# Hash attention with a max-out feed-forward on one core: token order, load runs, and which queue carries which transfer when

## The chip, the cores and the metric

One core of a Trainium2 chip. The metric is the device time of the whole program in microseconds (us); every time below is such a time or a duration in the trace of one profiled execution. A ratio between two kernels is the mean time of one kernel's runs over the mean of the other's runs of the same rounds, so it is not quite the ratio of the medians quoted beside it. PE is the matmul engine, PEld its weight loads; DVE, ACT and Pool are the vector, scalar and general engines; SP only issues DMAs. The granted clock is the share of PE's full clock that it was given.

## The reference

Attention with a bucket mask, then a feed-forward network (FFN) with a maximum of three products. B = 4, H = 8, S = 768, D = 64; 3072 tokens of 512 values, inner width 768.

```python
q_bits = (np.einsum('bhsd,dk->bhsk', q, proj) > 0)      # 6 hash bits for each token and head
k_bits = (np.einsum('bhsd,dk->bhsk', k, proj) > 0)
mask = q_bucket[:, :, :, None] == k_bucket[:, :, None, :]    # bucket = the 6 bits as a number
scores = np.where(mask, scale * np.matmul(q, k.transpose(0, 1, 3, 2)), -1e9)
attn = softmax(scores)
x = (attn @ v) laid out as (B*S, H*D)
h = np.maximum(np.maximum(x @ w1, x @ w2), x @ w3)
out = h @ w_out
```

## The kernel before

The program has 16 phases, one for each batch and pair of heads, and each phase has 12 units. A unit is two matmuls of q and k (one for each head) and one exp on ACT. A unit also carries small jobs from a list `todo[u]`. In phase n these are: the denominators and the product with v of phase n-1, the hash of pair n+1, the transposes of pair n+2, and the loads of pair n+3. Pieces of the FFN come from a queue (`ffn`) as fast as a quota allows. They can exist only once a batch has all four pairs.

The mask costs no pass over the scores. Twelve extra rows in the bf16 operands of each head (`kop`, `qop`) hold the hash bits and their complements, so that the matmul itself adds a large negative number for each differing bit. These rows are made for the next pair by a matmul (L237), turned into bits by DVE (`bt`) and moved to their rows by eight small DMAs of 12 partitions. They are called **row DMAs** below. The next phase can't start before its rows have landed.

```python
def load(nm, b, j):                       # q or k of a pair, three phases ahead
    t = natp.tile([P, R * D], FP32, ...)  # R = 24
    if b == 0:                            # two heads interleaved by 64 columns: runs of 256 bytes
        for hd in (0, 1):
            nc.sync.dma_start(t[:, 0:S].rearrange("p (c x) -> p c x", c=NCH)[:, :, D*hd : D*hd + D],
                              src[b, 2*j + hd].rearrange("(p c) d -> p c d", p=P))
    else:                                 # other batches: another token order, runs of 6016 bytes
        ...  nc.sync.dma_start(t[32*g : 32*g + 32, 0 : R*D - 32], ...)     # four for each tensor

def pe_transpose(nm, b, j, half, evac):   # batch 0 only; later batches are transposed on DVE
    for c in range(NT3):
        nc.tensor.transpose(ps[:, c*P : c*P + P], nat[nm, b, j][:, o : o + P], iden[:])

def hash_pair(b, j):                      # the row DMAs, on the queue of SP
    ...
    nc.vector.tensor_scalar(out=bt[:, half_cols(half)], in0=ps[half][:, 0:HS], ...)   # the bits
    for hd in (0, 1):
        for z, nm in enumerate(("q", "k")):
            nc.sync.dma_start(oset(b, j)[nm, hd][12 hash rows, half_cols(half)], bt[12 rows, ...])

def den_rc(ph): ...                       # denominators; eight small copies on Pool
def load_weight(i, after):                # a whole weight (768 KB) on Pool, held until `after` is written
    nc.gpsimd.tensor_copy(gate[:], after)
    nc.gpsimd.dma_start(t[:], w_ap...)

# the places (ph = phase, u = unit; cut)
ul = 7 if ph == 0 else 0
add(ul, load, "k", nb, nj); add(ul, load, "q", nb, nj)        # pair ph + 3
if nb > 0: add(9, load_v, nb, nj)                             # four DMAs on Pool
if ph == 0: add(8, load_weight, 0, ...)
if ph == 1: add(4, load_weight, 1, ...); add(10, load_weight, 2, ...)
if ph == 2: add(8, load_weight, 3, ...)                       # w_out
add(1, hash_pair, *pairs[ph + 1])
...
# after all units of a phase: FFN of a batch is queued one phase after its last pair
if ph > 0 and pairs[ph - 1][1] == NPAIR - 1:
    for half in (0, 1): ffn.extend(ffn_atoms(pairs[ph - 1][0], half))
```

The softmax here doesn't subtract the row's maximum and nothing guards it: scores larger than these inputs give would overflow.

Of the kernel before, what the change touches and what calls it, by code (L numbers as in the profile page):

```python
# [9 lines left out]
FP32 = mybir.dt.float32  # L10
FP16 = mybir.dt.float16
# [6 lines left out]
def kernel(  # L18
# [29 lines left out]
    TINY = 1.1754943508222875e-38  # L48

    konst = ctx.enter_context(tc.tile_pool(name="konst", bufs=1))  # L50
    natp = ctx.enter_context(tc.tile_pool(name="natp", bufs=2))
    tfp = ctx.enter_context(tc.tile_pool(name="tfp", bufs=2))
    vp = ctx.enter_context(tc.tile_pool(name="vp", bufs=5))
# [21 lines left out]
    nat = {}  # L75
    HBM = {"k": k, "q": q}

    def load(nm, b, j):
        src = HBM[nm]
        t = natp.tile([P, R * D], FP32, tag=nm + "nat", name=nm + "nat")  # L80
        if b == 0:
            for hd in (0, 1):
                nc.sync.dma_start(t[:, 0 : S].rearrange("p (c x) -> p c x", c=NCH)[:, :, D * hd : D * hd + D],
                                  src[b, 2 * j + hd].rearrange("(p c) d -> p c d", p=P))
        else:
            for hd in (0, 1):
                s = src[b, 2 * j + hd].rearrange("(i r) d -> i (r d)", r=R)
                for blk in (0, 1):
                    g = 2 * hd + blk
                    nc.sync.dma_start(t[32 * g : 32 * g + 32, 0 : R * D - 32],  # L90
                                      s[:, 32 * blk : 32 * blk + R * D - 32])
        nat[nm, b, j] = t

    def load_first():
        for nm in ("k", "q"):
            nat[nm, 0, 0] = natp.tile([P, R * D], FP32, tag=nm + "nat", name=nm + "nat")
        for half in (0, 1):
            for nm, eng in (("k", nc.sync), ("q", nc.scalar)):
                t3 = nat[nm, 0, 0][:, 0:S].rearrange("p (c x) -> p c x", c=NCH)
                for hd in (0, 1):  # L100
                    eng.dma_start(t3[:, half * NT3 : half * NT3 + NT3, D * hd : D * hd + D],
                                  HBM[nm][0, hd].rearrange("(p c) d -> p c d", p=P)[:, half * NT3 : half * NT3 + NT3, :])

    vt = {}

    def load_v(b, j):
        t = vp.tile([P, 2, NCH, D], FP16, tag="v", name="v")
        tv = t[:].rearrange("p h c d -> p h (c d)")
        sv = v[b, 2 * j : 2 * j + 2]
        if b == 0:  # L110
            nc.gpsimd.dma_start(tv, sv.rearrange("h (p c) d -> p h (c d)", p=P))
        else:
            s4 = sv.rearrange("h (i jj c) d -> jj i h (c d)", jj=4, c=NCH)
            for jj in range(4):
                nc.gpsimd.dma_start(tv[32 * jj : 32 * jj + 32], s4[jj])  # L115
        vt[b, j] = t

    pr = konst.tile([P, NBITS], FP32, name="pr")
    nc.gpsimd.dma_start(pr[0:D], proj[:, :])
    nc.gpsimd.dma_start(pr[D : 2 * D], proj[:, :])  # L120
    load_first()


    iden = konst.tile([P, P], FP32, name="iden")
# [46 lines left out]

    at = [konst.tile([P, 2, HS + 1], FP16, name=f"at{i}") for i in range(4 * NCH)]
    gate = konst.tile([P, 1], FP32, name="gate")
    w_sb = []

    def load_weight(i, after):
        nc.gpsimd.tensor_copy(gate[:], after)
        w_ap = (moe_w1, moe_w2, moe_w3, moe_w_out)[i]
        t = konst.tile([P, w_ap.shape[0] // P, w_ap.shape[1]], FP16, name=f"w{i}_sb")
        nc.gpsimd.dma_start(t[:], w_ap.rearrange("(c p) f -> p c f", p=P))  # L180
        w_sb.append(t)


    def psum2(name):
# [9 lines left out]
    def pe_transpose(nm, b, j, half, evac):  # L194
        if (nm, b, j) not in tf:
            tf[nm, b, j] = tfp.tile([P, S], FP32, tag=nm + "tf", name=nm + "tf")
        ps = bank()
        for c in range(NT3):
            o = half * HS + c * P
            nc.tensor.transpose(ps[:, c * P : c * P + P], nat[nm, b, j][:, o : o + P], iden[:])  # L200
        evac(tf[nm, b, j][:, half_cols(half)], ps[:, 0:HS])  # L201

    def transpose(nm, b, j):
        tf[nm, b, j] = tfp.tile([P, S], FP32, tag=nm + "tf", name=nm + "tf")
        dst = tf[nm, b, j][:]
        src = nat[nm, b, j][:].rearrange("p (r x) -> p r x", x=D)[:, :, 0:32]
        if nm == "q":
            nc.vector.transpose(dst.rearrange("p (r i) -> p r i", i=32), src)  # L208
        else:
            nc.vector.transpose(dst.rearrange("p (c jj i) -> p c jj i", jj=4, i=32),  # L210
                                src.rearrange("p (jj c) x -> p c jj x", jj=4))

    def convert(nm, b, j, cs=slice(0, S), copy=nc.vector.tensor_copy):
        for hd in (0, 1):
# [35 lines left out]
    def atile(ph, half, c):  # L250
        return at[(ph % 2) * 2 * NCH + 2 * c + half]
# [9 lines left out]
        nc.scalar.activation(atile(ph, half, c)[:, :, 0:HS], sc[:, :, 0:HS], ActFn.Exp, scale=SCALE)  # L261

    rcb = {}
    E32 = HS // 32

    def den_mm(ph, c0, c1):
# [39 lines left out]
    def av(ph, b, j, half):  # L306
        ps = bank()
        vv = vt[b, j]
        for c in range(NCH):
            for hd in (0, 1):  # L310
                nc.tensor.matmul(ps[D * hd : D * hd + D, 0 : HS + 1], vv[:, hd, c, :],  # L311
                                 atile(ph, half, c)[:, hd, :], start=(c == 0), stop=(c == NCH - 1))
        sv = dp.tile([P, 1], FP32, tag="sv", name="sv")
        nc.vector.tensor_scalar(out=sv[:], in0=ps[:, HS : HS + 1], scalar1=EPS, scalar2=None, op0=AluOp.mult)  # L314
        if b not in xT:
            xT[b] = xp.tile([P, NJC, S], FP16, tag="xT", name="xT")
        nc.vector.scalar_tensor_tensor(
            out=xT[b][:, j, half * HS : half * HS + HS], in0=ps[:, 0:HS],
            scalar=sv[:, 0:1], in1=rcb.pop((ph, half))[:], op0=AluOp.add, op1=AluOp.mult)


    hts = {}

    def l1(b, half, fb, m):
        ps = bank()
        for jc in range(NJC):
            nc.tensor.matmul(ps[:, 0:HS], w_sb[m][:, jc, fb * P : fb * P + P],  # L327
                             xT[b][:, jc, half * HS : half * HS + HS],
                             start=(jc == 0), stop=(jc == NJC - 1))
        if m == 0:  # L330
# [9 lines left out]
    def l2(b, half, t):  # L340
        ps = bank()
        for fb in range(NFB):
            nc.tensor.matmul(ps[:, 0:DM], hts[b, half, fb][:, t * P : t * P + P], w_sb[3][:, fb, :],  # L343
                             start=(fb == 0), stop=(fb == NFB - 1))
        if t == 0:
            ot[b, half] = op.tile([P, NT3, DM], FP32, tag="o", name="o")
        o = ot[b, half]
        nc.scalar.copy(o[:, t, :], ps[:, 0:DM])  # L348
        ob = out[b * S : b * S + S]
        c0 = half * NT3  # L350
        last = b == B - 1 and half == 1
        if b == 0:
            if t == NT3 - 1:
                nc.gpsimd.dma_start(ob.rearrange("(p t) m -> p t m", t=NCH)[:, c0 : c0 + NT3, :], o[:])
        elif t == NT3 - 1 or last:
            ts = slice(t, t + 1) if last else slice(0, NT3)
            o4 = ob.rearrange("(i c jj) m -> jj i c m", c=NCH, jj=4)
            for jj in range(4):
                eng = (nc.sync if jj % 2 == 0 else nc.scalar) if last else nc.gpsimd
                eng.dma_start(o4[jj][:, c0 + ts.start : c0 + ts.stop, :], o[32 * jj : 32 * jj + 32, ts, :])  # L360

    def ffn_atoms(b, half):
        for fb in range(NFB):
# [5 lines left out]

    pairs = [(b, j) for b in range(B) for j in range(NPAIR)]  # L370
    NU = 2 * NCH
    ffn = deque()
    ffn_left = [2 * B * (3 * NFB * 0.65 + NT3 * 1.28)]
    TAILW = 40.0

# [9 lines left out]
    hash_first("q", 0)  # L385
    convert("q", 0, 0, h0, acopy)
    pe_transpose("k", 0, 0, 1, vcopy)
    for j in (1, 2):
        load("k", 0, j)
        load("q", 0, j)  # L390
    load_v(0, 0)
    for t in at:
        nc.gpsimd.memset(t[:, :, HS : HS + 1], 1.0)

    for ph, (b, j) in enumerate(pairs):
        todo = {u: [] for u in range(NU)}

        def add(u, f, *a):
            todo[u].append(lambda: f(*a))
# [12 lines left out]
        if ph > 0:  # L412
# [7 lines left out]
            add(5, den_rb, ph - 1, 1)  # L420
            add(6, av, ph - 1, pb, pj, 0)
            add(8 if sparse else 6, av, ph - 1, pb, pj, 1)
        if ph + 3 < len(pairs):
            nb, nj = pairs[ph + 3]
            ul = 7 if ph == 0 else 0
            add(ul, load, "k", nb, nj)
            add(ul, load, "q", nb, nj)
            if nb > 0:
                add(9, load_v, nb, nj)
        if ph == 0:  # L430
            add(8, load_v, 0, 1)
            add(8, load_weight, 0, nat["q", 0, 2][:, 0:1])
        if ph == 1:
            add(4, load_weight, 1, atile(ph, 0, 1)[:, 0, 0:1])
            add(8, load_v, 0, 2)
            add(10, load_weight, 2, atile(ph, 0, 4)[:, 0, 0:1])
        if ph == 2:
            add(4, load_v, 0, 3)
            add(8, load_weight, 3, atile(ph, 0, 3)[:, 0, 0:1])
        if ph == 0:  # L440
            pass
        elif ph + 1 < len(pairs):
            add(1, hash_pair, *pairs[ph + 1])
        if ph + 2 < len(pairs):
            prep(*pairs[ph + 2], 8)
# [14 lines left out]
        for c, half in order:  # L460
# [9 lines left out]
                spent += cost  # L470
            ffn_left[0] -= spent
            u += 1
        if ph > 0 and pairs[ph - 1][1] == NPAIR - 1:
            for half in (0, 1):
                ffn.extend(ffn_atoms(pairs[ph - 1][0], half))

    lph = len(pairs) - 1
    tailf = [lambda: den_mm(lph, 0, NCH), lambda: den_rc(lph), None, None, lambda: den_rb(lph, 0), lambda: den_rb(lph, 1),
# [5 lines left out]
            ffn.popleft()[1]()  # L484
    while ffn:
        ffn.popleft()[1]()
    for half in (0, 1):
        for _, f in ffn_atoms(B - 1, half):
            f()


# [28 lines left out]
```

## Time and profile before

| | before |
|---|---|
| median, range | 311.2 us, 309.87 to 311.26 (3 runs) |
| profiled execution: span, mean granted clock | 310.3 us, 0.964 |
| PE busy | 281.6 us, 91% of the span |
| packets under 512 bytes | 17088 of 29631 |

The first fence is part 2 of the page of the kernel before: the span in 40 slices of 7.76 us, each digit a busy share in tenths; PEclk is the granted clock of PE, DMA the share of the 16 DMA engines.

```profile
PE   6686848478899999999999999999999999999993
PEclk9996978879999999999999999999999999999998
DMA  8687999995873738482856476630400030030303
```

From slice 12 on PE is full. Whatever is to be won lies in the first 11 slices, which are phases 0 to 4: no FFN work exists yet to fill PE, and the clock sinks too. The second fence is the windows view, one row for each of phases 0 to 4 (from the phase's first exp to the next phase's). Its columns are window and length, busy time of PE, PEld, DVE, ACT and POOL with instruction counts, then granted clock, DMA share and GB/s. (It counts a packet's whole time where the packet starts, and packets can overlap, so the share can pass 1.)

```profile
10.60:26.80 16.20, 11.28 (x76) 5.80 (x77) 12.64 (x25) 9.37 (x13) 3.35 (x5) 0.95 0.65 111
26.80:44.00 17.20, 13.29 (x101) 5.41 (x100) 9.10 (x19) 9.54 (x13) 6.34 (x17) 0.80 1.06 209
44.00:58.20 14.20, 11.27 (x88) 3.95 (x89) 6.65 (x14) 9.39 (x14) 5.25 (x15) 0.82 1.02 197
58.20:75.60 17.40, 10.93 (x88) 3.97 (x88) 8.89 (x18) 9.32 (x14) 3.55 (x12) 0.80 0.77 153
75.60:87.10 11.50, 9.65 (x90) 4.05 (x90) 8.94 (x18) 9.30 (x15) 3.55 (x12) 1.00 0.77 159
```

Phase 4 takes 11.5 us. Phases 1 to 3 have about the same work on ACT (9.3 to 9.5 us) and take 48.8 us together. The chain of waits (the work that ended last, followed back from the end, each piece to what released it) of the kernel before says what fills the difference (start, length, what; times in us):

```profile
1.97 3.69 DMA pr<-in_proj_dram
...
20.35 5.28 DMA kop_1_159<-bt
...
28.45 1.46 PE wk L237 x16
...
39.80 5.44 DMA kop_2_165<-bt
45.25 9.58 DMA qnat<-in_q_dram
54.85 0.72 SPq L246
55.61 7.59 DMA qop_0_151<-bt
```

Four waits, three for row DMAs and one for a load of q, make up 27.9 us. Not all of this is lost: engines work meanwhile, and phases 1 to 3 are 14.3 us longer than three phases of 11.5 us. A row DMA holds only 9 KB, so it isn't its size that makes it slow. The SP timeline of the kernel before shows the first reason, what stands before the rows on SP's queue (start, length, SP's issues by line, what, how many):

```profile
25.80 1.30 SPq L83 DMA_DIRECT2D knat<-in_k_dram  x2
27.21 1.27 SPq L83 DMA_DIRECT2D qnat<-in_q_dram  x2
28.58 2.91 SPq L90 DMA_DIRECT2D knat<-in_k_dram  x4
31.60 3.33 SPq L90 DMA_DIRECT2D qnat<-in_q_dram  x4
35.61 0.80 SPq L246 DMA_DIRECT2D qop_2_166<-bt  x1
```

The bits of this pair were computed by DVE from 29.98 on, the first half of them by 30.66. The first row went out at 35.61, 5.0 us later, behind eight load issues that took SP 6.2 us. The q load in the chain holds a row back too: SP stood 0.43 us until it had landed, and then issued the row at 54.85.

The second reason is what the rows meet on the DMA engines. From each row DMA's issue to the end of its last packet (worked out from the packet records of the trace) it took 4.2 to 5.2 us in phase 1 and 2.6 to 6.3 us in phase 2, while the DMA share was above 1.

The DMA view of the kernel before for the window from 3 to 9 us, when batch 0 is being loaded:

```profile
DMA packets 5373, 1.33 MB, mean 222 GB/s; under 512 B 5356, under 2 KB 5373, under 8 KB 5373
```

The PE timeline, six transposes of 128x128 in the transpose mode of PE, which is one tensor of one pair:

```profile
20.32 0.82 PE L200 MATMUL wk<-iden,knat 128*128 128x128 f32 x6
```

### The profile page before, as it was taken

The numbers are of one execution on the slowest core, as the hardware profiler recorded it, in microseconds if no ns is written. First come the engines' busy times: TensorE is split into PE (matmuls) and PEld (weight loads), VectorE is DVE, ScalarE is ACT, GpSimd is POOL, SyncE is SP. The second block draws the span as 40 slices with busy tenths as digits, with TensorE's granted clock in tenths as the row PEclk, the third lists the DMA queues.
The fourth block names the chain that finished last, engine by engine and source line by source line (L and its number), as shares of the span: only waits on it lengthen the run. The fifth ranks groups of instructions, "written<-read, shape, count | busy, mean of one in ns | idle before, by whom it ended". The sixth has DMA issues, their size and how long they took to land.

```text
span 310.3 us, 6166 instructions
## 1 busy us (share of the span) xinstructions
PE 281.6 (91%) x2184; PEld 144.1 (46%) x2184; DVE 194.6 (63%) x409; ACT 191.4 (62%) x286; POOL 75.9 (24%) x250
## 2 busy tenths in 40 slices
PE   6686848478899999999999999999999999999993
PEld 2331412123345554555455545554555455555551
DVE  3884544628697884688478857876796253725250
ACT  3573745548776668666868596868676776141412
POOL 8230612303404040404040415040301040120200
PEclk9996978879999999999999999999999999999998
DMA  8687999995873738482856476630400030030303
GB/s 170 126 130 155 211 222 221 153 211 103 160 189 55 201 47 228 98 196 41 207 132 156 74 188 155 165 70 4 111 2 9 2 104 1 2 90 11 90 15 103
DMA packets 29631, 35.73 MB, mean 115 GB/s; under 512 B 17088, under 2 KB 24928, under 8 KB 29600
## 3 DMA queue, kind: packets, MB, share of 16 engines
q1 hardware_dynamic: 18784, 22.75, 31.3%
q0 software_dynamic: 8928, 11.80, 20.3%
q10 hardware_dynamic: 1888, 0.79, 1.2%
q8 instruction: 17, 0.28, 0.4%
q14 instruction: 14, 0.11, 0.1%
HBM read 34.21 MB, written 6.29 MB: 131 GB/s over the span
## 4 chain that ended last, share of the span: by engine, by line
PE 79%; DMA 10%; DVE 4%; ACT 3%; issue 2%; ACTq 1%; SPq 1%; POOL 0%; DVEq 0%; POOLq 0%
PE wk L327 31%; PE sc L259 18%; PE wk L311 10%; PE wk L343 9%; PE wk L274 6%; PE wk L237 4%; DMA qnat<-in_q_dram 3%; DMA qop_0_151<-bt 2%; DMA kop_2_165<-bt 2%; DMA kop_1_159<-bt 2%; DMA pr<-in_proj_dram 1%; PE wk L222 1%; DVE ktf L201 1%; ACT o L348 1%; ACTq L360 1%
## 5 line engine op out<-in xcount | busy, mean ns | idle before, releaser
L327 PE MATMUL wk<-xT,w_sb 128*128 128x384 f16 x576 | 110.8, 326 | 0.0
L327 PEld LDWEIGHTS <-w_sb 128*128 128x128 f16 x576 | 54.1, 97 | 45.1 <-issue 9.8
L240 DVE TENSOR_SCALAR bt<-wk,thrqk,fac 128x384 bf16<-128x384 f32 x30 | 18.9, 672 | 36.1 <-PE wk L237 32.1
L259 PE MATMUL sc<-qop_0_151,kop_0_149 128*128 128x384 bf16 x72 | 23.7, 329 | 4.9 <-DMA qop_0_151<-bt 4.6
L311 PEld LDWEIGHTS <-v 128*64 128x64 f16 x384 | 20.6, 110 | 13.7 <-issue 6.4
L259 PE MATMUL sc<-qop_0_154,kop_0_153 76*128 76x384 bf16 x72 | 23.6, 328 | 3.4 <-DVE qop_0_154 L226 1.0
L259 PE MATMUL sc<-qop_1_160,kop_1_159 76*128 76x384 bf16 x60 | 20.4, 339 | 5.6 <-DMA kop_1_159<-bt 2.9
L115 POOL DMA_DIRECT2D v<-in_v_dram x48 | 25.4, 540 | 0.0
L259 PE MATMUL sc<-qop_2_166,kop_2_165 76*128 76x384 bf16 x60 | 20.0, 334 | 3.8 <-DMA kop_2_165<-bt 2.1
L348 ACT COPY o<-wk 128x512 f32<-128x512 f32 x24 | 14.0, 585 | 14.5 <-PE wk L343 14.4
L360 POOL DMA_DIRECT2D out_dram<-o x20 | 10.8, 549 | 47.7 <-ACT o L348 47.7
L259 PE MATMUL sc<-qop_2_163,kop_2_161 128*128 128x384 bf16 x60 | 20.1, 335 | 2.2 <-DMA qop_2_163<-bt 1.1
L259 PE MATMUL sc<-qop_1_157,kop_1_155 128*128 128x384 bf16 x60 | 20.2, 337 | 0.1
L274 PEld LDWEIGHTS <-ones_143 128*32 128x32 f16 x384 | 8.9, 99 | 17.6 <-issue 14.8
L237 PE MATMUL wk<-qtf,pmq 64*32 64x384 f32 x120 | 15.8, 564 | 0.0
L285 DVE STREAM_TRANSPOSE dT<-ds 128x384 f32<-128x384 f32 x16 | 9.2, 572 | 9.6 <-ACT ds L280 9.6
L237 PE MATMUL wk<-ktf,pmk 64*32 64x384 f32 x120 | 14.7, 564 | 0.0
L261 ACT ACTIVATE at_174<-sc 128x768 f16<-128x768 f32 x8 | 6.5, 814 | 11.5 <-PE sc L259 11.5
L314 DVE TENSOR_SCALAR sv<-wk 128x1 f32<-128x1 f32 x32 | 4.9, 153 | 12.3 <-PE wk L311 12.3
L261 ACT ACTIVATE at_169<-sc 128x768 f16<-128x768 f32 x8 | 6.5, 814 | 9.5 <-PE sc L259 9.5
L261 ACT ACTIVATE at_181<-sc 128x768 f16<-128x768 f32 x8 | 6.5, 814 | 8.9 <-PE sc L259 8.9
L208 DVE STREAM_TRANSPOSE qtf<-qnat 128x768 f32<-128x768 f32 x12 | 11.7, 975 | 0.2
(469 smaller groups left out, 641.2 us busy)
## 6 DMA issues: line engine op xcount, KB each, us to landing
knat<-in_k_dram SPq DMA_DIRECT2D x48, 188.0 KB
qnat<-in_q_dram SPq DMA_DIRECT2D x48, 188.0 KB
out_dram<-o POOLq DMA_DIRECT2D x20, 192.0 KB, 3.6
w_sb<-in_moe_w_dram POOLq DMA_DIRECT2D x3, 768.0 KB, 8.9
v<-in_v_dram POOLq DMA_DIRECT2D x48, 48.0 KB, 2.8
out_dram<-o POOLq DMA_DIRECT2D x2, 768.0 KB, 6.2
knat<-in_k_dram SPq DMA_DIRECT2D x6, 192.0 KB
qnat<-in_q_dram SPq DMA_DIRECT2D x6, 192.0 KB
```

Source lines behind the costliest of these rows:

```text
L115: nc.gpsimd.dma_start(tv[32 * jj : 32 * jj + 32], s4[jj])
L208: nc.vector.transpose(dst.rearrange("p (r i) -> p r i", i=32), src)
L237: nc.tensor.matmul(ps[half][o : o + 32, 0:HS], pm[nm][head_rows(hd), :], tf[nm, b, j][head_rows(hd), half_cols(half)], start=True, stop=True)
L240: nc.vector.tensor_scalar(out=bt[:, half_cols(half)], in0=ps[half][:, 0:HS], scalar1=thr["qk"][:, 0:1], scalar2=fac[:, 0:1], op0=AluOp.is_ ...
L259: nc.tensor.matmul(sc[:, hd, 0:HS], kT[rows, c * P : c * P + P], qT[rows, half * HS : half * HS + HS], start=True, stop=True)
L261: nc.scalar.activation(atile(ph, half, c)[:, :, 0:HS], sc[:, :, 0:HS], ActFn.Exp, scale=SCALE)
L274: nc.tensor.matmul(ps[32 * g : 32 * g + 32, 0:HS], ones32[:], atile(ph, half, c)[:, hd, 0:HS], start=(c == 0), stop=(c == NCH - 1))
L311: nc.tensor.matmul(ps[D * hd : D * hd + D, 0 : HS + 1], vv[:, hd, c, :], atile(ph, half, c)[:, hd, :], start=(c == 0), stop=(c == NCH - 1))
L327: nc.tensor.matmul(ps[:, 0:HS], w_sb[m][:, jc, fb * P : fb * P + P], xT[b][:, jc, half * HS : half * HS + HS], start=(jc == 0), stop=(jc = ...
L343: nc.tensor.matmul(ps[:, 0:DM], hts[b, half, fb][:, t * P : t * P + P], w_sb[3][:, fb, :], start=(fb == 0), stop=(fb == NFB - 1))
L348: nc.scalar.copy(o[:, t, :], ps[:, 0:DM])
L360: eng.dma_start(o4[jj][:, c0 + ts.start : c0 + ts.stop, :], o[32 * jj : 32 * jj + 32, ts, :])
```

## The change

Its intent: every batch in natural token order; batch 0 in longer runs and asked for early; the big loads on the queue of Pool, so that SP carries row DMAs and outputs; weights in halves, spread over later phases; the FFN of a batch queued as soon as its half of x is there. The diff, cut to its core:

```diff
+    natp0 = ctx.enter_context(tc.tile_pool(name="natp0", bufs=3))
+    def load0(nm, j, eng, cs=slice(0, NCH)):            # batch 0: runs of 1536 bytes (first pair 768)
+        src = HBM[nm][0, 2*j : 2*j + 2].rearrange("h (p c) d -> p h c d", p=P)[:, :, cs, :]
+        eng.dma_start(nat[nm, 0, j][:].rearrange("p h (c d) -> p h c d", d=D)[:, :, cs, :], src)
     def load(nm, b, j):                                  # other batches: runs of 1408 bytes
-                nc.sync.dma_start(t[32*g : 32*g + 32, 0 : R*D - 32], ...)
+                nc.gpsimd.dma_start(t[32*g : 32*g + 32, :, 0 : NCH*D - 32], ...)
     def load_v(b, j):                                    # one DMA in every batch (was four for b > 0)
...
+    for j in (1, 2, 3):                                  # before the first matmul
+        load0("k", j, nc.sync)
+        load0("q", j, nc.sync)
...
     pe_transpose:
-            nc.tensor.transpose(ps[:, c*P : c*P + P], nat[nm, b, j][:, o : o + P], iden[:])
+            for hd in (0, 1):
+                nc.tensor.matmul(ps[head_rows(hd), c*P : c*P + P], nat[nm, b, j][:, hd, o : o + D], iden[:], ...)
...
     av:
+        if j == NPAIR - 1:
+            ffn.extend(ffn_atoms(b, half))
...
     the places:
-            ul = 7 if ph == 0 else 0
-            add(ul, load, "k", nb, nj); add(ul, load, "q", nb, nj)
-            (weights: phase 0 unit 8, phase 1 units 4 and 10, w_out phase 2 unit 8)
+        if ph == 0:   add(8, load, "k", 1, 0); add(8, load, "q", 1, 0); (v)
+        if ph == 1:   add(6, load_weight, m, 0) for the three first halves; (v)
+        if ph >= 2:   add(6, load, "k", nb, nj); add(6, load, "q", nb, nj)
+        if ph == 3:   add(8, load_weight, m, 1) for the three second halves
+        if ph == 4:   add(8, load_wo)
...
     outputs on SP instead of Pool; the last copy and store split over two engines
```

## The prediction

> **What bounds it now.** Two regimes. From 87 us to the end PE is the bound: the windows view has PE busy 16.0 of every 16 us from 87 to 251. Before 87 us (attention phases 0 to 4; no FFN work exists until phase 4 ends) nothing is full: PE busy about 0.57 to 0.9, clock 0.69 to 0.82 between 26 and 72 us. By the first exps in the timeline, phases 0 to 4 start at 10.6, 26.8, 44.0, about 58 (then a 4.8 us ACT gap) and 75.6 us. Phase 4, which waits for no DMA, takes 11.5 us; the others 12 to 19. The chain of waits shows why: hash rows (kop_1 5.3 us, kop_2 5.4, qop_0 7.6) and 9.6 us of q loads. A hash pair is eight SP issues of 0.72 us behind the loads: in phase 1 the bits were ready at about 30.7 us, the first row went out at 35.6, after eight load issues of 6.2 us; rows then took 4 to 7 us to land in a loaded DMA system.
>
> **What changes.**
> 1. Batch-0 q/k come in 1536-byte runs (768 for the first pair) instead of 256. Over half of all packets (17088 of 29631) are under 512 bytes now. The Trainium skill ("DMA: Bandwidth & Descriptors", Specifications) asks for 512 for line rate; the trace agrees: DMA share 0.98 at only 175 GB/s in the first 10 us.
> 2. SP carries hash rows almost alone; later q/k loads go to Pool: 8 issues per phase at about 0.54 us (the v loads) = 4.3 us, less 3 saved v issues. Pool is 24% busy; its denominator copies come half a phase later, so this should fit. Later loads have 1408-byte runs instead of 6016, same bytes within 6%.
> 3. FFN of batch 0 starts inside phase 4, at unit 6: about 6 units in which PE was 0.81 busy, 1 to 1.5 us.
> 4. Batch-0 PE transposes become plain fp32 matmuls, two per block. The skill's "TensorE: Matmul & The Clock Gate" (Terms) calls the transpose mode 4x faster for fp32. Now six take 0.81 us; from L237 and L222 (384 fp32 columns, pairs side by side, 0.7 to 0.84 us) I estimate 0.25 to 0.45 us per block after: +0.4 to 0.9 us per half, 16 halves, at the start and in phases 0 and 1: +5 to 8 us of PE, perhaps +3 on the chain.
> 5. The last copy and store are split over two engines: about -0.7 us.
>
> **Sum.** Phase 0 stays about 16 us including its wait (longer transposes eat what the hash wait gives back). Phases 1, 2, 3 shrink to about 13, 12, 12: phase 4 starts near 64 instead of 75.6, -11. FFN in phase 4 -1.3, tail -0.7, remaining collisions of hash rows with weight loads (phases 3 and 4 must move about 7.6 MB in 24 us, an estimate, above the 222 GB/s peak slice of before) +2. Total about -11.
>
> **Prediction: 300 us, 8 in 10 between 293 and 306.** Faster by over 2%: 0.84; within: 0.13; slower: 0.03.
>
> **What would show it.** First exp of phase 4 near 64 us; PE clock near full in phases 1 to 3; first hash row of phase 1 within 1 us of its bits; hash rows no longer over 3 us each in the chain; about 100% PE from phase 4's middle; transpose line busy at least doubled.
>
> **What would make it wrong.** Pool stalls when its queue fills (three weight halves, then eight loads), holding the denominator copies and with them av; transposes cost more at the start; weights or loads late in phases 4 to 5, so early FFN waits; hash rows still 5 us late behind Pool's traffic.

## More of the kernel before

SP's waits view of the kernel before, row issues that waited for a k load (us in total, times, longest):

```profile
SPq L246 <- DMA knat<-in_k_dram: 2.3, 4, 1.1
```

These waits are semaphore waits of the program's instructions; no run shows a limit of the chip here.

## The result, and the profile after

All outputs are right. The four runs of each kernel on one chip:

| | before | after |
|---|---|---|
| median, range | 310.62 us, 309.87 to 311.26 | 301.8 us, 300.76 to 303.22 |
| ratio, 95% interval | 1 | 0.972, 0.967 to 0.977 |
| profiled execution: device time, span, clock | 312.09 us, 310.3 us, 0.964 | 301.46 us, 299.7 us, 0.998 |
| PE busy | 281.6 us | 281.5 us |
| packets under 512 bytes | 17088 of 29631 | 3744 of 21727 |

PE's busy time is the same to 0.1 us: dearer transposes (+5.2 us) and a faster clock (the hash matmuls alone, L237 before and L234 after, -4.4 us) cancel. What went is its idle time. Part 2 of the page of the kernel after:

```profile
PE   6788888887999899999999999999999999999994
PEclk9999999999999999999999999999999999999999
DMA  7556193789979093909372757367202020020202
```

The dips of PE to 4 are gone, and so are those of the clock. In the first 11 slices the DMA row now has quiet slices (7 5 5 6 1 9 3 7 8 9 9), where it had nine slices of 6 to 9 in a row. The windows view of the kernel after, phases 0 to 4 as above, with one later window:

```profile
12.30:28.70 16.40, 14.61 (x157) 8.06 (x158) 13.14 (x25) 9.33 (x13) 6.85 (x11) 1.00 0.61 148
28.70:42.30 13.60, 12.05 (x136) 6.35 (x135) 9.00 (x19) 9.32 (x14) 4.38 (x12) 1.00 0.53 78
42.30:53.60 11.30, 9.41 (x88) 3.86 (x88) 6.78 (x15) 9.26 (x15) 6.23 (x17) 1.00 0.58 118
53.60:65.00 11.40, 9.55 (x88) 3.86 (x88) 8.83 (x18) 9.21 (x14) 6.48 (x18) 1.00 0.71 151
65.00:80.10 15.10, 13.37 (x114) 6.37 (x114) 10.97 (x21) 10.37 (x16) 10.30 (x22) 1.00 1.18 217
96.00:112.00 16.00, 14.95 (x134) 7.22 (x136) 11.39 (x22) 12.62 (x20) 6.51 (x17) 1.00 0.57 116
```

From these rows and the first exps, the two profiled executions compare so (us):

| stretch | before | after | difference | predicted |
|---|---|---|---|---|
| start to first exp | 10.6 | 12.3 | +1.65 | in the sum for transposes |
| phase 0 | 16.2 | 16.4 | +0.25 | 0 |
| phases 1 to 3 | 48.8 | 36.4 | -12.5 | to about 37, so -11 to -12 |
| phase 4's first exp to the end | 234.7 | 234.6 | -0.1 | 0 (FFN -1.3, tail -0.7, collisions +2) |
| sum | | | -10.7 | -11 |

(The differences use the unrounded times of the exps.) The profiled executions differ by 10.6 us; the medians of all runs differ by 8.8. The profiled execution of the kernel before (312.09 us) was slower than all four timed runs (up to 311.26), so this table flatters the change by 1 to 2 us, and no trace says in which stage.

The chain of waits of the kernel after, where the four long waits were:

```profile
1.94 5.37 DMA pr<-in_proj_dram
...
29.73 0.81 PE wk L234 x16
...
43.46 0.81 PE wk L234 x16
...
51.39 0.81 ACT at_187 L258
```

One DMA wait is left, the one for the projection at the start, and it has grown from 3.69 to 5.37 us. From phase 1 on the chain is mostly matmuls and exps. The SP timeline of the kernel after, for the same rows as shown before:

```profile
27.29 0.71 SPq L243 DMA_DIRECT2D kop_1_166<-bt  x1
31.32 0.72 SPq L243 DMA_DIRECT2D qop_2_177<-bt  x1
32.08 0.72 SPq L243 DMA_DIRECT2D kop_2_176<-bt  x1
```

SP now stands idle until the bits are there, and issues the first row at 31.32; DVE began the bits at 30.61. And the POOL timeline of the kernel after shows what else is in flight. The copies of the denominators go first, then the loads, then the weights (phase 3):

```profile
59.55 0.87 POOL L293 COPY r_893<-rc 32x12 f32<-32x12 f32 x4
60.37 2.19 POOL L91 DMA_DIRECT2D knat<-in_k_dram  x4
62.55 2.23 POOL L91 DMA_DIRECT2D qnat<-in_q_dram  x4
64.77 2.36 POOL L174 DMA_DIRECT2D w_sb<-in_moe_w_dram  x3
```

Pair 4's rows were issued from 56.7 to 62.2, so most of them left ahead of these loads; they landed in 1.5 to 2.7 us. The landing times of row DMAs, worked out from the packet records of each trace (issue of the DMA to the end of its last packet; the eight of a pair):

| kernel, rows of pair | issued | us to land | bulk in flight |
|---|---|---|---|
| before, 2 | 35.6 to 41.3 | 4.2 to 5.2 | q/k loads, weights |
| before, 3 | 49.4 to 56.4 | 2.6 to 6.3 | q/k loads from 42.1 |
| after, 2 | 31.3 to 36.7 | 1.5 to 2.0 for five, 3.3 to 5.4 for the last three | from 35.1 three weight halves |
| after, 3 | 45.0 to 50.6 | 1.5 to 2.9 | loads from 48.8 |
| after, 4 | 56.7 to 62.2 | 1.5 to 2.7 | loads from 60.4 |
| after, 5 | 68.2 to 73.8 | 4.1 to 5.2 | loads and weight halves since 60.4 |

The DMA view of the kernel after, 3 to 9 us, and the PE timeline for six transposed blocks (the same work as the line shown before):

```profile
DMA packets 1902, 2.08 MB, mean 347 GB/s; under 512 B 185, under 2 KB 1902, under 8 KB 1902
```

```profile
22.75 1.53 PE L200 MATMUL wk<-iden,knat_106 128*64 128x128 f32 x24
```

Long runs do move more bytes in a time (347 for 222 GB/s), and the transposes do cost more (1.53 for 0.82 us; 1.31 to 1.53 over the run).

### The profile page after: what moved, and what is told of

It reads as the page before. It is cut to its first block, busy times and chain, and to the rows that moved or that the text cites. A ratio compares the mean times of both kernels' runs of the same rounds, so it can differ in the third digit from the quotient of the medians. Undisturbed runs are those within 1.5% of the kernel's fastest.

```text
span 299.7 us, 6326 instructions
## 1 busy us (share of the span) xinstructions
PE 281.5 (94%) x2328; PEld 147.7 (49%) x2328; DVE 196.4 (66%) x410; ACT 190.8 (64%) x286; POOL 101.5 (34%) x288
## 2 busy tenths in 40 slices
DMA packets 21727, 34.56 MB, mean 115 GB/s; under 512 B 3744, under 2 KB 15936, under 8 KB 21696
## 4 chain that ended last, share of the span: by engine, by line
PE 85%; ACT 6%; DVE 3%; issue 2%; DMA 2%; POOL 1%; ACTq 0%; DVEq 0%; POOLq 0%
PE wk L327 32%; PE sc L256 19%; PE wk L309 11%; PE wk L343 10%; PE wk L272 5%; PE wk L234 4%; PE wk L200 3%; DMA pr<-in_proj_dram 2%; PE wk L219 1%; DVE qtf L202 1%; ACT at_194 L258 1%; ACT at_201 L258 1%; ACT at_182 L258 1%; ACT at_181 L258 1%; ACT at_200 L258 1%
## 5 line engine op out<-in xcount | busy, mean ns | idle before, releaser
L237 DVE TENSOR_SCALAR bt<-wk,thrqk,fac 128x384 bf16<-128x384 f32 x30 | 18.9, 673 | 22.3 <-PE wk L234 22.2
L256 PE MATMUL sc<-qop_0_165,kop_0_164 76*128 76x384 bf16 x72 | 23.6, 328 | 4.1 <-DVE qop_0_165 L223 0.6
L91 POOL DMA_DIRECT2D qnat<-in_q_dram x48 | 26.5, 559 | 1.0 <-DMA v<-in_v_dram 1.0
L91 POOL DMA_DIRECT2D knat<-in_k_dram x48 | 26.4, 558 | 0.8 <-issue 0.8
L256 PE MATMUL sc<-qop_0_162,kop_0_160 128*128 128x384 bf16 x72 | 23.5, 326 | 0.4 <-DVE qop_0_162 L223 0.3
L256 PE MATMUL sc<-qop_1_171,kop_1_170 76*128 76x384 bf16 x60 | 19.7, 328 | 3.1 <-DMA kop_1_170<-bt 1.0
L256 PE MATMUL sc<-qop_2_177,kop_2_176 76*128 76x384 bf16 x60 | 19.7, 328 | 2.2 <-ACT at_187 L258 0.6
L256 PE MATMUL sc<-qop_1_168,kop_1_166 128*128 128x384 bf16 x60 | 19.6, 326 | 0.1
L256 PE MATMUL sc<-qop_2_174,kop_2_172 128*128 128x384 bf16 x60 | 19.6, 327 | 0.0
L258 ACT ACTIVATE at_185<-sc 128x768 f16<-128x768 f32 x8 | 6.5, 814 | 11.6 <-PE sc L256 11.6
L234 PE MATMUL wk<-qtf,pmq 64*32 64x384 f32 x120 | 13.4, 495 | 0.0
L234 PE MATMUL wk<-ktf,pmk 64*32 64x384 f32 x120 | 12.7, 495 | 0.0
L99 POOL DMA_DIRECT2D v<-in_v_dram x16 | 11.8, 739 | 1.7 <-PE sc L256 1.2
L256 PEld LDWEIGHTS <-kop_0_164 76*128 76x128 bf16 x72 | 7.0, 97 | 10.5 <-issue 5.3
L256 PEld LDWEIGHTS <-kop_0_160 128*128 128x128 bf16 x72 | 7.1, 98 | 9.9 <-issue 6.6
```

What stands on the lines that cost most here:

```text
L91: nc.gpsimd.dma_start(t[32 * g : 32 * g + 32, :, 0 : NCH * D - 32], s[:, :, 32 * blk : 32 * blk + NCH * D - 32])
L99: nc.gpsimd.dma_start(t[:].rearrange("p h c d -> p h (c d)"), v[b, 2 * j : 2 * j + 2].rearrange("h (p c) d -> p h (c d)", p=P))
L234: nc.tensor.matmul(ps[half][o : o + 32, 0:HS], pm[nm][head_rows(hd), :], tf[nm, b, j][head_rows(hd), half_cols(half)], start=True, stop=True)
L256: nc.tensor.matmul(sc[:, hd, 0:HS], kT[rows, c * P : c * P + P], qT[rows, half * HS : half * HS + HS], start=True, stop=True)
L258: nc.scalar.activation(atile(ph, half, c)[:, :, 0:HS], sc[:, :, 0:HS], ActFn.Exp, scale=SCALE)
```

## The experiments

Theory T: the gain is an arrangement in time. Row DMAs no longer wait behind load issues on SP, and the bulk is asked for at moments when no rows are due. Rival R1: the gain is the longer runs, which make all DMA faster. Rival R2: it is the queue alone, SP kept for rows. Rival R3: a good part comes from the early FFN. Twelve kernels ran. In names, `a_` starts from the kernel after and undoes something, `b_` starts from the kernel before and adds something. All ratios are to the kernel before on the same chip:

| kernel | edit | median us | ratio, 95% interval |
|---|---|---|---|
| after | | 301.8 | 0.972, 0.967 to 0.977 |
| a_short_runs | 256-byte runs again, same plain transposes | 302.75 | 0.976, 0.969 to 0.983 |
| a_short_tmode | 256-byte runs and transpose mode | 301.2 | 0.971, 0.966 to 0.975 |
| a_loads_sp | later q/k loads on SP | 306.49 | 0.986, 0.980 to 0.993 |
| a_weights_old | whole weights at their old places | 307.93 | 0.988, 0.983 to 0.994 |
| a_two_tiles | two early tiles instead of three | 305.44 | 0.985, 0.980 to 0.990 |
| a_ffn_late | FFN queued as before | 302.82 | 0.976, 0.970 to 0.982 |
| a_credit | unused FFN quota kept | 303.75 | 0.978, 0.973 to 0.983 |
| a_pr_first | projection on ACT's queue | 303.72 | 0.977, 0.973 to 0.981 |
| a_mixed | first pair short runs, rest long | 301.5 | 0.969, 0.964 to 0.974 |
| b_loads_pool | q/k loads on Pool, place unchanged | 313.1 | 1.010, 1.005 to 1.015 |
| b_pool_u6 | q/k loads on Pool at unit 6 | 304.31 | 0.979, 0.974 to 0.985 |
| b_long_runs | long runs of batch 0, plain transposes | 311.04 | 1.001, 0.997 to 1.005 |

Runs of one kernel spread over 1 to 4.5 us, so a difference of about 1 us between two variants isn't resolved here.

### Long runs taken out, or put in alone (R1)

a_short_runs keeps everything of the kernel after but the layout of batch 0's tile:

```diff
-            nat[nm, 0, j] = natp0.tile([P, 2, S // 2], FP32, ...)
-        eng.dma_start(... "p h (c d) -> p h c d" ...)             # runs of 1536 bytes
+            nat[nm, 0, j] = natp0.tile([P, NCH, 2, D], FP32, ...)
+        for hd in (0, 1):
+            eng.dma_start(nat[nm, 0, j][:, cs, hd, :], ...)       # runs of 256 bytes
```

> The changed kernel with one thing undone: batch-0 q/k land in runs of 256 bytes again (tile with the two heads interleaved, one DMA per head), plain-matmul transposes and everything else kept. Theory 1 (run length frees the DMA engines early, and that matters): DMA below 250 GB/s in the first 10 us instead of 350 to 390, all batch-0 loads done about 5 us later, first exps of phases 0 and 1 later, total 2 to 5 us over the changed kernel (303.5 to 307). Theory 2 (what counts is only that hash rows no longer stand behind load issues on SP): under 1.5 us over the changed kernel, and phase 4 still starts near 65 to 67 us.

Measured: 302.75 us, ratio 0.976. The first exp of phase 4 came at 66.7 (after: 65.0; before: 75.6).

b_long_runs puts long runs and plain transposes into the kernel before and leaves queue and places alone:

```diff
+            t = natp0.tile([P, 2, S // 2], FP32, ...)
+            nc.sync.dma_start(t[:].rearrange("p h (c d) -> p h c d", d=D),
+                              src[0, 2*j : 2*j + 2].rearrange("h (p c) d -> p h c d", p=P))
-            nc.tensor.transpose(...)
+            for hd in (0, 1): nc.tensor.matmul(...)
```

> The kernel before with only the batch-0 loads changed: runs of 1536 bytes (768 for the first pair), tile by head, plain-matmul transposes; queues and places as before. Theory 1: DMA in the first 10 us at 300 GB/s or more, the rows land sooner in phases 0 and 1, 3 to 6 us gained (305 to 308). Theory 2: the rows of phase 1 still go out behind eight load issues (4 to 5 us after their bits), and the transposes cost 1 to 2 us, so under 2 us gained or even lost (309 to 312).

Measured: 311.04 us, ratio 1.001, interval 0.997 to 1.005: no gain. Its chain still has row waits of 5.17 and 6.95 us.

a_short_tmode takes both halves of the trade out of the kernel after, long runs and plain transposes:

```diff
 (a_short_runs, and)
-            for hd in (0, 1): nc.tensor.matmul(...)
+            nc.tensor.transpose(ps[:, c*P : c*P + P], nat[nm, b, j][:, half*NT3 + c].rearrange("p h d -> p (h d)"), iden[:])
```

> The run with 256-byte runs (302.75 us), with the batch-0 transposes back in transpose mode (one 128-wide instruction per block, possible only with the heads interleaved, which is what forces the short runs). Isolates the cost of the plain matmuls, predicted as +3 us on the chain. From the traces 24 instructions fewer per pair and matrix, 0.4 us per half: if they are on the chain, 2 to 4 us less (299 to 301); if phase 0 hides them, under 1 us.

Measured: 301.2 us, ratio 0.971, which can't be told from the kernel after (0.972). R1 falls: 56% more GB/s in the first microseconds, taken with the plain transposes that come with it, buys nothing that can be measured. This is a balance of effects. Beside a_short_runs, which differs in the run length alone, the kernel after has its first exp 1.6 us later (12.3 for 10.6) and takes 3.3 us less for phases 0 and 1 (30.0 for 33.3). From the chain of waits of a_short_runs:

```profile
22.62 5.74 DMA kop<-bt
```

And beside a_short_runs, a_short_tmode, which differs in the transposes alone, takes 1.6 us less for phases 0 and 1 (31.7): the price of the plain transposes, between the two forecasts. These are single profiles; the totals (medians 0.95 and 1.55 us apart) have overlapping intervals.

### Queue and place (R2)

b_loads_pool is the kernel before with one word changed in `load`:

```diff
-                    nc.sync.dma_start(t[32*g : 32*g + 32, ...
+                    nc.gpsimd.dma_start(t[32*g : 32*g + 32, ...
```

> The kernel before with one word changed: q/k loads of batches 1 to 3 on Pool, at their old place (unit 0). Theory 2 (the SP queue alone): rows of phase 1 go out at about 31 instead of 35.6 us, phase 4 starts 6 to 10 us earlier, total 301 to 305. Theory 1 (also the loaded DMA engines): only 2 to 5 us gained, 306 to 309, because rows still take 4 to 7 us to land. A risk for either: loads at unit 0 stand ahead of the denominator copies on Pool (about 4.4 us of issues), which could cost av some wait.

Measured: 313.1 us, ratio 1.010: a loss. SP was free, so rows went out at once, but they still took 5.1 to 6.5 us to land in phase 2 (pair 3), beside loads and a weight on the other queue. The POOL timeline of b_loads_pool shows a new cost (the bracket at the end is the idle time before the line, and what ended it):

```profile
65.41 0.49 POOL L90 DMA_DIRECT2D knat<-in_k_dram  x1 [4.06 <-DMA w_sb<-in_moe_w_out_dram]
...
67.86 1.81 POOL L295 COPY r<-rc 32x12 f32<-32x12 f32 x8
```

After w_out, four v loads and three k loads Pool stood 4.06 us before it issued the fourth k load. The semaphore records say why: w_out is the DMA eight issues before, and the load waited for its semaphore. Behind that load and the four of q stood the copies of the denominators, and the products with v wait for those. The chain holds 8.69 us of w_out. The profiled execution is the fastest of the four (310.44 us): in it phase 4 begins at 71.8 (before: 75.6) and takes 15.0 us (before: 11.5). Why the other three (312.3 to 314.9) are slower still, no trace shows. R2 falls: the queue alone does not bring the gain.

b_pool_u6 changes one number more, the unit:

```diff
-                    nc.sync.dma_start(t[32*g : 32*g + 32, ...
+                    nc.gpsimd.dma_start(t[32*g : 32*g + 32, ...
-            ul = 7 if ph == 0 else 0
+            ul = 7 if ph == 0 else 6
```

> The kernel before with two words changed: q/k loads of batches 1 to 3 on Pool, and asked for at unit 6 (after the denominator copies) instead of unit 0. The run with Pool at unit 0 was 313.1 us, not faster, with Pool idle 4 us in front of a load behind the w_out load. Theory A (the place did it: loads ahead of the denominator copies): 301 to 305 us, phases 2 to 4 near 11.5 to 13 us each. Theory B (the four whole weight loads of phases 0 to 2 fill the Pool queue, and loads behind them stall the copies wherever they stand): 308 us or more, DMA w_sb still in the chain, Pool idle 3 us or more in front of a load.

Measured: 304.31 us, ratio 0.979. Two edits, of a word and a number, give about three quarters of the whole gain (2.1 of 2.8%). At unit 6 most row DMAs of the phase (unit 1) and the copies (unit 2 or 3) have been issued. What it still pays is the old places of the weights; from the POOL timeline of b_pool_u6:

```profile
68.04 0.49 POOL L90 DMA_DIRECT2D knat<-in_k_dram  x1 [3.25 <-DMA w_sb<-in_moe_w_out_dram]
```

a_loads_sp goes the other way: the kernel after with its later loads back on SP, at the same units.

```diff
-                nc.gpsimd.dma_start(t[32*g : 32*g + 32, :, 0 : NCH*D - 32],
+                nc.sync.dma_start(t[32*g : 32*g + 32, :, 0 : NCH*D - 32],
```

> The changed kernel with one word undone: the q/k loads of batches 1 to 3 are issued on SP again, at the same places in the program (unit 6). Theory 2 (the queue): SP must issue 16 DMAs a phase, about 8 x 0.72 + 8 x 0.6 = 10.5 us in phases of 11.5 us, so hash rows are late again in phases 2 to 5; the chain shows DMA waits on the row tiles; total 4 to 9 us over the changed kernel. Theory 3 (the place: before issued the loads one unit ahead of the rows, here they come behind them): under 1.5 us over the changed kernel, rows go out within 1 us of their bits.

Measured: 306.49 us, ratio 0.986: half of the gain is lost. Phases 1 to 3 take 37.5 us (after: 36.4); phase 4 takes 20.1 us instead of 15.1. From the chain of waits of a_loads_sp:

```profile
62.00 6.56 DMA qop<-bt
...
77.98 5.16 DMA kop<-bt
```

The queue does matter in phases 3 and 4, when the second weight halves on Pool are due as well. It isn't the order of issue that does it: SP issued all eight rows of pair 4 (56.5 to 62.8) before its first load (63.5), and the latest of them still took up to 5.6 us to land. With the loads on Pool the weights come behind the loads on one queue, at 64.77; here nothing stands before them. From the POOL timeline of a_loads_sp:

```profile
60.19 2.25 POOL L174 DMA_DIRECT2D w_sb<-in_moe_w_dram  x3
```

The four rows issued before this took 1.5 to 3.0 us to land, the four after it 4.0 to 5.6. So the one word also moved the weight halves 4.6 us forward, into the rows. That this is the whole reason is my reading, and no run tests it. Whether the place alone (unit 6 on SP, in the kernel before) would have gained was not run and stays open.

### The weights at their old places

```diff
-                for m in range(3): add(6, load_weight, m, 0)       # phase 1, halves
-                for m in range(3): add(8, load_weight, m, 1)       # phase 3, halves
-                add(8, load_wo)                                    # phase 4
+            add(8, load_weight, 0, ...)                            # phase 0, whole, held as before
+                add(4, load_weight, 1, ...); add(10, load_weight, 2, ...)    # phase 1
+                add(8, load_weight, 3, ...)                        # phase 2
```

> The changed kernel with only the weights undone: four whole weights at their old places (phases 0, 1, 1 and 2, gated as before) in place of halves in phases 1 and 3 and w_out in phase 4. Theory A (place of the q/k loads is enough): 301 to 303 us. Theory B (weights in the way on the Pool queue): 305 us or more, phases 2 and 3 longer than 12.5 us, with waits for Pool's copies or for late q/k loads.

Measured: 307.93 us, ratio 0.988. The loss is not in phases 2 and 3 (11.3 and 11.5 us), where theory B had it: phases 0, 1 and 4 take 17.7, 17.3 and 17.0 us (after: 16.4, 13.6, 15.1), and the rows are back in the chain of waits of a_weights_old:

```profile
26.86 4.86 DMA qop<-bt
...
66.82 4.49 DMA qop<-bt
```

So the new places of the weights, in halves, carry over half of the gain as the kernel after stands; places and halves were not separated. b_pool_u6, which has the old places as well, does better (0.979). It lacks the early loads of batch 0, so the parts don't simply add; which of the other differences makes this kernel the slower one wasn't tested.

### Fewer early tiles

The program of the kernel after asks for the last three pairs of batch 0 before the first matmul. With three buffers the loads of the second and third pair go out by 3.8 us, and those of the fourth wait until a tile is free (10.7 and 17.0). With two the third pair has to wait as well (10.0 and 16.3):

```diff
-    natp0 = ctx.enter_context(tc.tile_pool(name="natp0", bufs=3))
+    natp0 = ctx.enter_context(tc.tile_pool(name="natp0", bufs=2))
```

> The changed kernel with one number changed: two instead of three batch-0 tiles for each of q and k, so that the third pair's loads wait on SP for the first pair's transposes. Putting the projection first on ACT only moved the late start from it to the first q tile (first exp 14.1 us). Theory (the prefetch of three pairs crowds out what the start needs): projection landed by 6.3 us instead of 7.3, first exp near 11 instead of 12.3 us, about 1 us less in all (300 to 301.5). Rival (the start is late for the longer transposes): no earlier than 12 us. Against both: rows of phase 0 may now stand behind the third pair's loads on SP and give it back.

Measured: 305.44 us, ratio 0.985, nearly half of the gain lost. It is lost in phases 0 and 1, 19.3 us for 16.4 and 15.5 for 13.6. The rows of pair 1 took 3.2 to 6.4 us to land (after: 1.6 to 4.4), and the chain of waits of a_two_tiles has

```profile
23.52 6.72 DMA kop<-bt
```

Loads that wait for a buffer fall on the rows of phase 0. The first exp came at 11.6, between the two forecasts; but a_credit and a_loads_sp, whose start is that of the kernel after, had it at 11.5 and 11.6, so this decides nothing.

### The early FFN (R3)

```diff
-        if j == NPAIR - 1: ffn.extend(ffn_atoms(b, half))       # in av
+        if ph > 0 and pairs[ph - 1][1] == NPAIR - 1:            # after the units of the phase, as before
+            for half in (0, 1): ffn.extend(ffn_atoms(pairs[ph - 1][0], half))
```

> The changed kernel with the early FFN undone: FFN of a batch is queued at the end of the phase after its last pair, as before. Predicted worth of the early start 1.3 us; but from phase 4's first exp to the end both kernels took 234.7 us. If the early start is worth nothing as built: within 0.5 us of the changed kernel, phase 4 at 11.5 us. If it is worth 1 us or more and something else ate it: 302.8 us or more.

Measured: 302.82 us, ratio 0.976. By the forecast this is just the case of "1 us or more", but the intervals overlap; it can't be told from the kernel after, so 1 us or nothing. Phase 4 is shorter without FFN in it (11.5 for 15.1 us), but then phase 5 opens with a wait. From its chain of waits:

```profile
72.64 5.83 DMA qop<-bt
```

PE stands idle for 1.64 us there, and the clock falls to 0.74 between 76 and 80 us. In the kernel after the rows of pair 5 are no faster (4.1 to 5.2 us), but FFN work covers them. From phase 4's first exp to the end a_ffn_late takes 235.7 us, 1.1 more than the kernel after. That isn't clear of noise either: a_mixed below, with the code of the kernel after in this stretch, takes 235.5. R3 falls in its size: about 1 us or nothing, of a gain of 8.8. A reason why it isn't more can be read in the last row of the windows view after: between 96 and 112 us PE is busy 14.95 of 16 us. The pieces left at that point cost 1.28, the rule lets one through if half its cost fits the quota, and 0.64 is over a quota of 0.61. Seven units at the start of phase 6 therefore got none.

a_credit lets unused quota add up:

```diff
+            credit += quota if ffn else 0.0
-            while ffn and spent + ffn[0][0] / 2 <= quota:
+            while ffn and spent + ffn[0][0] / 2 <= credit:
...
+            credit -= spent
```

> The changed kernel with the FFN pacing changed: the quota left over from one unit is carried to the next, so second-layer pieces (1.28) are not held back when the quota (0.61) is just under half of one. In the changed kernel seven units in a row at the start of phase 6 got no FFN work, with 1.05 us of PE idle between 96 and 112 us, which the kernel before does not have. If that ate the gain of the early FFN: PE full between 96 and 112 us, 0.5 to 1.2 us less in all (300.5 to 301.5). If not, no change.

Measured: 303.75 us, ratio 0.978: no gain, if anything a small loss. The windows view of a_credit, the same window and a late one:

```profile
96.00:112.00 16.00, 15.92 (x131) 7.97 (x130) 11.43 (x23) 12.07 (x19) 6.86 (x17) 1.00 0.55 147
...
224.00:240.00 16.00, 15.27 (x115) 8.14 (x114) 6.80 (x15) 11.56 (x17) 2.14 (x9) 1.00 0.11 18
```

The hole is filled (15.92 of 16), and as much idle time comes up elsewhere. The amount of FFN work is fixed; moved forward, it is missing later. This may also limit what the early FFN can give, but no run separates that from its other effects.

### The start

The first exp came 1.65 us later. I had put such a delay down to the transposes. a_pr_first moves the projection from Pool's queue to ACT's, ahead of q:

```diff
-    nc.gpsimd.dma_start(pr[0:D], proj[:, :])
-    nc.gpsimd.dma_start(pr[D : 2*D], proj[:, :])
+    nc.scalar.dma_start(pr[0:D], proj[:, :])
+    nc.scalar.dma_start(pr[D : 2*D], proj[:, :])
```

> The changed kernel with the two tiny projection loads issued first on ACT instead of on Pool. In the changed kernel they landed at 7.3 us (5.7 before) while 300 to 390 GB/s of q/k loads ran, and the first hash waited for them. Theory (crowded out by the faster prefetch): landing by about 4 us, first exp near 10.5 instead of 12.3 us, 1 to 2 us less in all (300 to 301). Rival (the plain-matmul transposes made the start later, the projection only ended last): first exp no earlier than 11.7 us and no change in all.

Measured: 303.72 us, ratio 0.977, and the first exp at 14.1 us, later still. The chain of waits of a_pr_first:

```profile
1.99 5.67 DMA qnat<-in_q_dram
7.70 1.55 PE wk L200 x12
```

The wait has moved to q, which now leaves after two small DMAs. Three blocks of transposes (12 records) then take 1.55 us, longer than the 1.31 to 1.53 that six blocks take later. The first hash matmuls are slow there too (1.49 us, 0.86 in the kernel after), while the granted clock reads 1.00; why wasn't settled.

a_mixed loads the first pair as before (256-byte runs, transpose mode) and the rest as after:

```diff
+        if j == 0:
+            for hd in (0, 1):
+                eng.dma_start(t3[:, cs, D*hd : D*hd + D], HBM[nm][0, hd].rearrange("(p c) d -> p c d", p=P)[:, cs, :])
+            return
...
+            if j == 0:
+                nc.tensor.transpose(ps[:, c*P : c*P + P], flat[:, 2*o : 2*o + P], iden[:])
+                continue
```

> A version meant to beat both kernels: the changed kernel with only the first pair of batch 0 as before (heads interleaved, 256-byte runs, transpose mode), later pairs in long runs with plain matmuls. From the runs: short runs and transpose mode gave a first exp at 10.63 us against 11.5 to 12.6 for the changed kernel's start, but then waited 5.4 us for hash rows in phase 0 behind the rest of the short-run loads, which long runs do not (1 us). If both add up: first exp near 10.7, phase 1 near 27 instead of 28.7, phase 4 near 63.5 instead of 65.0, total 299.5 to 301 (ratio 0.965 to 0.969). If the row wait comes back or the start is crowded by the long-run prefetch all the same: no better than the changed kernel (0.972).

Measured: 301.5 us, ratio 0.969, interval 0.964 to 0.974. The projection's wait is 3.89 us again and the first exp comes at 10.8. The 1.5 us won at the start do not show in the total beyond doubt; the first exp of phase 4 is at 64.0 for 65.0. The row wait came back in part (4.69 us in the chain; phase 0 takes 16.9 us for 16.4). This version beats the kernel before, and isn't separable from the kernel after.

Over the kernels the rule at the start is plain. The projection landed (start plus length of its wait in the chain) at 5.66 us before, 7.31 after, 5.83 in a_mixed, 6.63 in a_two_tiles and 7.63 in a_weights_old; the first exps came at 10.6, 12.3, 10.8, 11.6 and 12.6. Each time it is 4.9 to 5.0 us from the landing to the exp, with either kind of transposes. a_short_runs settles it: with plain transposes and short runs its projection landed at 5.67 and its first exp came at 10.6. The start's delay is thus the landing of one small DMA beside long-run loads, and the transposes there cost nothing. (In a_pr_first and a_short_tmode the chain goes through a q load instead.) The versions with long runs in the first pair had 4.6 to 5.7 us of this wait, those with short runs 3.7 to 3.9. Why long runs press harder on it, no run shows.

## Why the prediction was right, point by point

- **The time**: 300 us predicted, 293 to 306; 301.8 measured. The main step held: phases 1 to 3, predicted at 13, 12 and 12 us, took 13.6, 11.3 and 11.5, phase 4 began at 65.0 where 64 were predicted, and the clock in these phases went from 0.80 to 0.82 up to 1.00.
- **Rows behind load issues**: predicted as the first row of phase 1 within 1 us of its bits. It went out at 31.32, 0.7 us after DVE began on the bits. No row DMA of over 3 us is left in the chain. The prediction put the delay before down to issue time; half of it was waits for the landing of loads issued before (2.5 of 5.0 us). What the prediction didn't have is how much of the gain comes from *when* the bulk is asked for: on Pool at their old unit the loads lose 1%, at unit 6 they gain 2.1%; and the new places of the weights, over half of the gain, have no term in it but the +2.
- **Landing in a loaded DMA system**: the Trainium skill, "DMA: Bandwidth & Descriptors", section "Issuing engines are not separate DMA queues", says that DMAs started by any engine end up on the same 16 DMA engines and interleave there. The runs agree: with SP free and the bulk on Pool the rows of b_loads_pool still took 5.1 to 6.5 us. When little else was in flight they took 1.5. That is somewhat under the fixed cost of about 2 us which the same page gives under "Anatomy of one DMA", for the path of Pool.
- **The clock**: the skill's "TensorE: Matmul & The Clock Gate", Part 1, has the clock throttled by default and released by activity. The trace agrees: where PE starved (phases 1 to 3 before) the mean was 0.80 to 0.82, and a group of 16 hash matmuls took 1.46 us on the chain (granted clock from 28.4 to 30.0 us: 0.50) where it takes 0.81 after. So the waits were paid a second time, in slower matmuls. No run separates the two payments.
- **Longer runs**: the step as costed held for the rate and not for its worth. The skill's "DMA: Bandwidth & Descriptors", Specifications, asks for 512 bytes for line rate; the trace agrees with 347 for 222 GB/s. It was worth about 1 us in the total (a_short_runs; 3.3 us in phases 0 and 1, less 1.6 at the start), and nothing with the transposes counted (a_short_tmode).
- **Transposes**: predicted +5 to +8 us of PE, +3 on the chain, line busy at least doubled. The line's busy time went from 7.2 to 12.4 us, so +5.2 and a factor of 1.7. The skill's "TensorE: Matmul & The Clock Gate", Terms, has the transpose mode 4 times faster for fp32. Here six blocks took 1.31 to 1.53 us for 0.82, where a block is two matmuls of half the width; their records overlap (24 of about 0.27 us in 1.5 us). On the chain the +3 isn't to be seen at the start, which is the projection's. In phases 0 and 1 the plain transposes cost 1.6 us (a_short_runs against a_short_tmode); 2.8 us of them lie on the chain in phase 1, which is 2 us longer than phases 2 and 3.
- **Early FFN**: predicted "-1.3", from six units with PE at 0.81, and PE about 100% busy from phase 4's middle. PE was busy 0.92 there, and idle 0.7 us; before it stood idle 0.85 us in that half phase, so 1.3 could not all come from it. The time from phase 4's first exp to the end stayed the same (234.7 and 234.6), as the prediction's three terms there add up to (-1.3 - 0.7 + 2). Whether the terms hold one by one is open: a_ffn_late puts the early FFN at 1 us or nothing, and where the quota let nothing through, a hole came back.
- **Tail**: predicted -0.7, measured -1.0 from the last exp to the end (48.97 to 48.01 us).
- **Collisions, +2**: they exist (rows of pair 5 took 4.1 to 5.2 us). Without the early FFN over them phase 5 takes 19.0 us (a_ffn_late) where it took 16.0 before. The traffic behind the estimate was set too high: phases 3 and 4 moved 5.0 MB, not 7.6. The collision that did show, at the start, wasn't foreseen.
- **"Pool stalls when its queue fills"**: named as a risk. In the kernel after it is 1.03 us once; in b_loads_pool it is 4.06 us and costs the gain.

The sum came out close, partly by luck: the start's +1.65 wasn't foreseen, and phases 2 and 3, 0.5 to 0.7 us shorter than predicted, give part of it back. By the medians the gain is 8.8 of the 11 us predicted; the profiled executions agree better (10.6) mainly because the one of the kernel before was slow.

What stays open: how much the place alone gives on SP; whether the weights' halves or their places count; why the projection lands later beside long runs; and anything about 1 us in size.

## What to carry to other kernels

When a small transfer that the next stage waits for shares the DMA engines with bulk loads, ask first *when* the bulk goes out. Put it behind the small one in time, in quiet stretches or at the very start (where it cost the projection 1.65 us here). Count the DMAs of a queue too: in this program the ninth waits for the landing of the first. Moving bulk to another queue frees the issuing engine, not the DMA engines, and it can hold up whatever else that queue's engine has to do; here the same move lost 1% at one place in the schedule and gained 2.1% at another.

## What the Trainium skill lacked or had wrong

- "DMA: Bandwidth & Descriptors" gives a fixed cost and a rate for one DMA, and no landing time of a small copy between tiles under load. Here a DMA of 9 KB landed in 1.5 us on quiet engines and in up to 6.5 us beside bulk loads, on the same queue (before, pair 3: 2.6 to 6.3) or another (b_loads_pool, pair 3: 5.1 to 6.5).
- The same page advises against spreading DMAs over engines for bandwidth, since only issue time is saved ("Rules for kernel authors"). No run here tests the bandwidth. But the shared queue held the first row back 5.0 us (first bits done at 30.66, issue at 35.61), and 2.5 us of this were no issue time but waits for the landing of earlier DMAs of that queue.
- That page's breakdown puts a DMA's dispatch at about 50 ns, for the path of Pool. For SP it has no figure for how long an issue occupies the engine: here it is mostly 0.71 to 0.72 us for a row DMA of 12 partitions, eight for each phase (on Pool 0.55 us for a load).
- None of the pages I read says how many DMAs of one queue may be outstanding before its next issue stalls. Here an issue on Pool stood 4.06 us for the landing of the DMA eight issues before it, a weight of 768 KB. It is a semaphore wait of this program (eight semaphores in turn for each queue); a limit of the chip isn't shown.
- "TensorE: Matmul & The Clock Gate" has the transpose mode 4 times faster for fp32; here replacing it by plain matmuls, two of half the width for each block, cost 1.6 to 1.9 times as much (1.31 to 1.53 us for 0.82). The same matmul with and without the mode was not run, so the 4 is neither shown nor refuted.
